# Short token blocks of a mixture-of-experts kernel: the second layer in two halves of 64 columns of the array

## The chip, the cores and the metric

The kernel runs on one core of a Trainium2 chip. The metric is the device time of one execution in microseconds. The core has five engines that run their own instruction streams and wait for each other by semaphores: TensorE (PE in the profile; its weight loads are PEld), VectorE (DVE), ScalarE (ACT), GpSimd (POOL) and SyncE (SP, which here only issues transfers). An engine's sequencer handles register loads, tests and jumps; the profile marks these with a q (PEldq, ACTq).

## What is computed

A linear attention feeds a mixture of experts with one expert per token. Softmaxes of q (over the head dimension) and of k (over the sequence) are multiplied with v; the 8 heads of 64 make rows x of 512. Each of the 8 x 576 = 4608 rows goes through one of 8 experts:

```
out = zeros((B, S, D))
for b in range(B):
    prev_e = -1
    for s in range(S):
        fresh_e = argmax(logits[b, s])
        e = fresh_e if s == 0 or local_gate[b, s] < 0.5 else prev_e
        prev_e = e
        p = softmax(logits[b, s])
        h = maximum(x[b, s] @ w1[e], 0)       # 512 -> 1024
        out[b, s] = p[e] * (h @ w2[e])        # 1024 -> 512
```

With this input five of the experts get rows, 1152, 576, 595, 576 and 1709 of them.

## The kernel before

The first part (to about 170 us) computes the attention and the choice of experts. Then the rows are sorted by expert on the chip and cut into blocks of at most 128 rows of one expert. A block whose expert has no more rows than 64 left is short; a word of the block's `info` says so. There are 38 blocks. Blocks 0 to 5 come from an order written out by hand (`ORDER`, `Plan`), the others from `block(b)` (line 1135), whose Python order is the order of each engine's instructions; the last ones lie in nested conditions (`rest`, line 1174).

Inputs and weights are split in two f16 parts each, high and low, and three products of the four are summed, so that the result is as good as f32. For a block, `gather` fetches the rows, `prep_x`, `prep_hi` and `prep_lo` scale and split them, and `turn_dma` transposes them by a transfer into `xT`. In `block(b)` these last steps work for block b + 3. `ffn1(b, g)`, for g = 0 and 1, makes half of the 1024 hidden values, transposed (`hidden`: 32 matmuls, tokens as columns). In blocks from 6 on it tests the word `few` on TensorE, and a short block streams half the columns. `act_copy`, `act_add`, `act_hi` and `act_lo` (ScalarE, VectorE, ScalarE, VectorE) apply the relu and split the hidden values into `hi` and `lo`. `ffn2(b, g)` (line 905) takes these as the stationary operand, 128 hidden values x 128 tokens, streams 512 columns of `w2h` or `w2l`, and sums 12 matmuls for each g into `py`, one bank of PSUM, of which there is one buffer. `give` (line 911, ScalarE) scales `py` by the row's share `pb` into `ys`, and `put` (POOL) scatters the rows to the output.

When block b + 1 belongs to a new expert, `renew` (line 953) splits that expert's weights, 16 pieces, each with one ScalarE and one VectorE instruction. It stands in a condition (line 954) in both engines' streams, between the steps above: pieces 0 to 9 during block b, 10 to 15 during block b + 1.

The order in `block(b)` that matters here is, with other work left out: `ffn1(b, 0)`, `act(b, 0)`, weight pieces, `ffn2(b - 1, 1)`, `ffn1(b, 1)`, `give(b - 1)`, `put(b - 1)`, weight pieces, `prep_hi` and `prep_lo` of block b + 3, `act(b, 1)`, weight pieces, `ffn2(b, 0)`. So `ffn2(b, 0)` waits until `give(b - 1)` has read `py`.

A condition that tests on one engine makes each other engine jump to the join as well; where two arms raise a semaphore by different counts, the arm with fewer is brought to the larger count.

Of the kernel before, what the change touches and what calls it, by code (L numbers as in the profile page):

```python
# [12 lines left out]
AF = mybir.ActivationFunctionType  # L13
ALU = mybir.AluOpType
AX = mybir.AxisListType
ET = mybir.EngineType
# [3 lines left out]
DM = H * D  # L20
# [11 lines left out]
NA = 6  # L32
# [117 lines left out]
def moe_kernel(ctx, tc, q, k, v, w_gate, w_local, w1, w2, out, dbg=None):  # L150
    nc = tc.nc
# [11 lines left out]
    W, plan = {}, []  # L163
# [3 lines left out]
    gidx, sidx, info = [], [], []  # L167
# [6 lines left out]
    def at(pair, b):  # L174

        return pair[0][:, b] if b < NA else pair[1][:, b - NA]
# [605 lines left out]
    xg, xn, x2, xT, pb, pt, py, hi, lo, hf, ys, ph = ([] for _ in range(12))  # L782
    fst, e0, few, phs = {}, {}, {}, {}
    AHEAD, NPB = 4, 4
# [36 lines left out]
    def word(w_, hi_, engines):  # L821
        return nc.values_load(w_, min_val=0, max_val=hi_, engines=engines,
                              skip_runtime_bounds_check_because="clamped where it is worked out")
# [39 lines left out]
    def ffn1(b, g):  # L863
        if b < NA:
            hidden(b, g, P)
            return
        if g == 0:
            few[0] = word(at(info, b)[:, 5:6], 1, [ET.PE])
        with tc.If(few[0] == 1) as cmp:
            hidden(b, g, P // 2)  # L870
        with cmp.Else():
            hidden(b, g, P)

    def hidden(b, g, n):

        ph_, xT_ = ph[g % len(ph)], xT[b % 4]
        phs[g] = ph_
        for f in range(4):
            fs = slice(P * (4 * g + f), P * (4 * g + f) + P)

            def big(c):
                nc.tensor.matmul(ph_[:, f, :].rearrange("p (i t) -> p i t", i=2)[:, :, 0:n], W["w1h"][:, c, fs], xT_[:, :, c, 0:n],  # L882
                                 start=(c == 0), stop=(c == 3))

            big(0)
            for c in range(4):
                nc.tensor.matmul(ph_[:, f, 0:n], W["w1l"][:, c, fs], xT_[:, 0, c, 0:n], start=False, stop=False)  # L887
            for c in range(1, 4):
                big(c)
# [13 lines left out]
                                       op0=ALU.max, op1=ALU.subtract)  # L903

    def ffn2(b, g):
        hi_, lo_ = hi[b % 2], lo[b % 2]
        for f in range(4 * g, 4 * g + 4):
            for i, (h_, w_) in enumerate(((hi_, W["w2h"]), (hi_, W["w2l"]), (lo_, W["w2h"]))):
                nc.tensor.matmul(py[0], h_[:, f, :], w_[:, f, :], start=(f == 0 and i == 0), stop=(f == 7 and i == 2))  # L909

    def give(b):
        nc.scalar.activation(ys[b % 2], py[0], AF.Copy, scale=pb[b % NPB])  # L912

    def put(b):
        i_, j_ = (sidx[0], b) if b < NA else (sidx[1], b - NA)
# [153 lines left out]
    for b in range(NP + 4):  # L1069
# [28 lines left out]
        for g in range(2):  # L1098
            wp_ = [("Wl", 4 * g + i) for i in range(4)] if b == 0 else [("RN", b, g)]
            add(("F1", b, g), PE, ffn1, after=[("Tc" if b < NT_PE else "D", b)] + wp_, order=[("ow",)] + ([("F2", b - 1, g)] if b else [("F1", 0, 0)] * g)  # L1100
                + ([("F1", b, 0)] if g else []), takes=[("psh", (b, g))], uses=[("xT", b)])
            add(("Ac", b, g), ACT, act_copy, after=[("F1", b, g)], uses=[("psh", (b, g))], takes=[("hf", (b, g))])
            add(("Ad", b, g), DVE, act_add, after=[("Ac", b, g)], uses=[("psh", (b, g)), ("hf", (b, g))])
            add(("Ar", b, g), ACT, act_hi, after=[("Ad", b, g)], uses=[("hf", (b, g))] + ([("hh", b)] if g else []), takes=[] if g else [("hh", b)])
            add(("Al", b, g), DVE, act_lo, after=[("Ar", b, g)], uses=[("hf", (b, g)), ("hh", b)])
            if b == NP - 1 and g:
                continue
            wp_ = [("Wl", 8 + 4 * g + i) for i in range(4)] if b == 0 else [("RN", b, 2 + g)]
            add(("F2", b, g), PE, ffn2, after=[("Al", b, g)] + wp_, order=[("F1", b, 1)] if g == 0 else [("F1", b + 1, 0)],
                takes=[] if g else [("psy", b)], uses=[("hh", b)] + ([("psy", b)] if g else []))  # L1110
        if b < NP - 1:
            add(("Gv", b), ACT, give, after=[("F2", b, 1), ("Gp", b)], uses=[("psy", b), ("pb", b)], takes=[("y", b)])
            add(("Pt", b), POOL, put, after=[("Gv", b)], uses=[("y", b)])
# [21 lines left out]
    def block(b):  # L1135
# [5 lines left out]
        if b + 1 < NBM:  # L1141
            gather_share(b + 1)
            if b + 1 not in fst:
                flag(b + 1)
        ffn1(b, 0)
        act(b, 0)
        renew(b, FROM[b][0])
        next_(b, (0, 1))
        ffn2(b - 1, 1)
        ffn1(b, 1)  # L1150
        give(b - 1)
        put(b - 1)
        renew(b, FROM[b][1])
# [3 lines left out]
        renew(b, FROM[b][2])  # L1157
        next_(b, (4, 5, 6, 7))
        ffn2(b, 0)
        next_(b, (8, 9))  # L1160
        if b + 3 < NBM:
# [24 lines left out]
    def last(b):  # L1186
        ffn2(b, 1)
        give(b)
        put(b)
# [29 lines left out]
```

## Time and profile before

| what | us |
|---|---|
| median of 3 runs | 592.33 |
| lowest and highest | 591.73, 595.31 |
| profiled execution, its time | 594.43 |
| profiled execution, its span | 592.6 |
| mean granted TensorE clock | 0.92 of full |

The span runs from the first to the last instruction. A row of a timeline gives the start from the span's begin, the duration, engine, line, operation, the tiles written and read, shapes as partitions x elements, how many instructions the row merges, and in square brackets how long the engine was idle before it and who ended that. Matmuls overlap, so their step is the difference of starts, not the duration. A granted clock of 1.00 is 2.4 GHz, 0.50 is 1.2 GHz.

### The profile page before, as it was taken

What the parts mean: (1) busy time and instruction counts of PE and PEld (TensorE: products, weight loads), DVE (VectorE), ACT (ScalarE), POOL (GpSimd) and SP (SyncE); (2) the same over time, 40 slices, a digit from 0 to 9 for tenths busy, and PEclk for the clock granted to TensorE, in tenths of its full rate; (3) what the DMA queues carried; (4) which work ended last, traced back from release to release, by engine and by line L of the source; (5) the groups of instructions that cost most, each with busy time, mean ns of one, the idle gap of its engine ahead of it and who ended that gap; (6) DMA issues with size and microseconds to landing.
All of it is one profiled execution on the core that took longest, in us unless ns stands there. A gap on an engine that the chain in (4) does not pass through costs nothing. (4 is left out here: it accounts for less than half of the span.)

```text
span 592.6 us, 15086 instructions
## 1 busy us (share of the span) xinstructions
PE 522.8 (88%) x5558; PEld 371.2 (63%) x5558; DVE 349.1 (59%) x626; ACT 266.2 (45%) x442; POOL 213.1 (36%) x230
## 2 busy tenths in 40 slices
PE   2667886877679999899999899999998999999995
PEld 2456665656556666476576666666665776667762
DVE  3687789889868886335743763474376333333331
ACT  1544345276447353235643743464375333333332
POOL 4132313223611212455344353443534434252441
PEclk9777789576769999799999999999999999999999
DMA  9999989997772454763895499369649924333341
GB/s 234 256 257 219 275 216 266 261 206 174 238 269 43 132 178 143 195 199 104 201 211 113 77 289 140 76 209 211 125 60 262 180 71 108 59 106 68 76 97 48
DMA packets 101297, 98.55 MB, mean 166 GB/s; under 512 B 56255, under 2 KB 84927, under 8 KB 101184
## 3 DMA queue, kind: packets, MB, share of 16 engines
q1 hardware_dynamic: 93536, 74.92, 53.4%
q0 software_dynamic: 7648, 22.20, 14.3%
q8 instruction: 62, 1.02, 0.8%
q14 instruction: 51, 0.42, 0.3%
HBM read 206.76 MB, written 20.89 MB: 384 GB/s over the span
## 5 line engine op out<-in xcount | busy, mean ns | idle before, releaser
L909 PE MATMUL py<-w2h,hi 128*128 128x512 f16 x304 | 116.2, 382 | 7.4 <-ACT y L912 3.5
L909 PE MATMUL py<-w2h,lo 128*128 128x512 f16 x304 | 116.3, 382 | 0.6
L909 PE MATMUL py<-w2l,hi 128*128 128x512 f16 x304 | 116.2, 382 | 0.2 <-DVEq L954 0.2
L882 PEld LDWEIGHTS <-w1h 128*128 128x128 f16 x1216 | 104.2, 98 | 14.3 <-issue 0.3
L916 POOL DMA_INDIRECT out<-y,sidx x38 | 39.2, 1032 | 195.5 <-ACTq L954 138.2
L887 PEld LDWEIGHTS <-w1l 128*128 128x128 f16 x1216 | 91.7, 98 | 14.3 <-issue 0.3
L909 PEld LDWEIGHTS <-hi 128*128 128x128 f16 x608 | 59.0, 98 | 65.7 <-issue 9.3
L882 PE MATMUL ph<-xT,w1h 128*128 128x256 f16 (+1 forms) x624 | 97.7, 270 | 0.0
L882 PE MATMUL pi<-xT,w1h 128*128 128x256 f16 (+1 forms) x592 | 91.8, 268 | 0.0
L902 DVE SCALAR_TENSOR_TENSOR lo<-hf,hi 128x512 f16<-128x512 f32 x76 | 54.8, 721 | 46.1 <-ACTq L954 37.6
L898 ACT ACTIVATE hi<-hf 128x512 f16<-128x512 f32 x76 | 47.8, 629 | 71.0 <-DVE hf L895 68.6
L895 DVE TENSOR_TENSOR hf<-ph,hf 128x512 f32<-128x512 f32 x39 | 26.9, 691 | 70.8 <-ACT hf L892 64.6
L847 DVE SCALAR_TENSOR_TENSOR x<-xn,x 128x512 f16<-128x512 f32 x41 | 35.0, 857 | 45.1 <-ACT x L184 43.5
L887 PE MATMUL ph<-xT,w1l 128*128 128x128 f16 (+1 forms) x624 | 59.6, 218 | 0.0
L892 ACT COPY hf<-ph 128x512 f32<-128x512 f32 x39 | 22.7, 582 | 80.9 <-PE ph L882 71.7
L887 PE MATMUL pi<-xT,w1l 128*128 128x128 f16 (+1 forms) x592 | 55.9, 217 | 0.0
L828 POOL DMA_INDIRECT xg<-xrows,gidx x42 | 45.3, 1077 | 29.2 <-issue 11.6
L909 PEld LDWEIGHTS <-lo 128*128 128x128 f16 x304 | 29.9, 98 | 39.6 <-DVE lo L902 2.4
L834 POOL DMA_INDIRECT pb<-shares,gidx x39 | 43.5, 1116 | 7.9 <-issue 7.6
L839 POOL TENSOR_TENSOR xn<-xg 128x512 f32<-128x512 f32 x35 | 37.3, 1067 | 16.7 <-DMA xg<-xrows,gidx 12.6
L410 POOL TENSOR_TENSOR qs<-qt,qm 128x512 f32<-128x512 f32 x23 | 24.9, 1094 | 49.7 <-DVE qm L404 18.1
L357 PE MATMUL pk<-VP,KT 128*64 128x65 f32 (+1 forms) x640 | 39.9, 280 | 2.7 <-issue 1.9
(223 smaller groups left out, 681.5 us busy)
## 6 DMA issues: line engine op xcount, KB each, us to landing
s<-in_moe_w SPq DMA_DIRECT2D x77, 2048.0 KB
xrows<-xt SPq DMA_DIRECT2D x12, 888.0 KB
qt<-in_q SPq DMA_DIRECT2D x24, 384.0 KB
KT<-in_k SPq DMA_DIRECT2D x16, 512.0 KB
VT<-in_v SPq DMA_DIRECT2D x16, 512.0 KB
s<-in_moe_w SPq DMA_DIRECT2D x4, 1024.0 KB
KT<-in_k SPq DMA_DIRECT2D x8, 128.0 KB
VT<-in_v SPq DMA_DIRECT2D x8, 128.0 KB
```

The source lines that it names most:

```text
L357: nc.tensor.matmul(pkv[64 * i:64 * i + 64, g], KT[b % NKT][ps, 4 * i + g, c], VP[b % 2][ps, 4 * i + g, c], start=(c == 0), stop=(c == KC - 1))
L828: nc.gpsimd.indirect_dma_start(out=xg[b % AHEAD], out_offset=None, in_=src, in_offset=bass.IndirectOffsetOnAxis(ap=i_[:, j_:j_ + 1], axis=0))
L834: nc.gpsimd.indirect_dma_start(out=pb[b % NPB], out_offset=None, in_=src, in_offset=bass.IndirectOffsetOnAxis(ap=i_[:, j_:j_ + 1], axis=0))
L839: eng.tensor_tensor(out=xn[b % 2].rearrange("p (g x d) -> p g x d", g=4, x=2), in0=xg[b % AHEAD].rearrange("p (g x) -> p g x", g=4)[:, :, ...
L847: nc.vector.scalar_tensor_tensor(out=x2[b % 2][:, 1, :], in0=xn[b % 2], scalar=XS, in1=x2[b % 2][:, 0, :], op0=ALU.mult, op1=ALU.subtract)
L882: nc.tensor.matmul(ph_[:, f, :].rearrange("p (i t) -> p i t", i=2)[:, :, 0:n], W["w1h"][:, c, fs], xT_[:, :, c, 0:n], start=(c == 0), stop ...
L887: nc.tensor.matmul(ph_[:, f, 0:n], W["w1l"][:, c, fs], xT_[:, 0, c, 0:n], start=False, stop=False)
L895: nc.vector.tensor_tensor(out=hf[g], in0=phs[g][:, :, 0:P], in1=hf[g], op=ALU.add)
L898: nc.scalar.activation(hi[b % 2][:, 4 * g:4 * g + 4, :], hf[g], AF.Relu)
L902: nc.vector.scalar_tensor_tensor(out=lo[b % 2][:, gs_, :], in0=hf[g], scalar=0.0, in1=hi[b % 2][:, gs_, :], op0=ALU.max, op1=ALU.subtract)
L909: nc.tensor.matmul(py[0], h_[:, f, :], w_[:, f, :], start=(f == 0 and i == 0), stop=(f == 7 and i == 2))
L916: nc.gpsimd.indirect_dma_start(out=outr, out_offset=bass.IndirectOffsetOnAxis(ap=i_[:, j_:j_ + 1], axis=0), in_=ys[b % 2], in_offset=None, ...
```

## The change

In a short block from block 6 on, `ffn2` becomes `result_few`: each matmul is split into two with the same 64 tokens as the stationary operand. One gives output columns 0 to 255 through columns 0 to 63 of the array into partitions 0 to 63 of `py`, the other output columns 256 to 511 through columns 64 to 127 into partitions 64 to 127. `give` then copies the second half from partitions 64 to 127 to the first 64 partitions of `ys`, scales the first half there, and scales the second in place: three ScalarE instructions. The word `few[b]` is now kept per block and loaded on ScalarE too, and `ffn2` (TensorE) and `give` (ScalarE) test it. Full blocks take the old instructions behind these tests. The description of the change also has "rows transposed three blocks ahead"; the diff is this:

```diff
--- before.py
+++ after.py
@@ -865,8 +865,8 @@
             hidden(b, g, P)
             return
         if g == 0:
-            few[0] = word(at(info, b)[:, 5:6], 1, [ET.PE])
-        with tc.If(few[0] == 1) as cmp:
+            few[b] = word(at(info, b)[:, 5:6], 1, [ET.PE, ET.Activation])
+        with tc.If(few[b] == 1) as cmp:
             hidden(b, g, P // 2)
         with cmp.Else():
             hidden(b, g, P)
@@ -903,13 +903,41 @@
                                        op0=ALU.max, op1=ALU.subtract)
 
     def ffn2(b, g):
+        if b < NA:
+            result(b, g)
+            return
+        with tc.If(few[b] == 1) as cmp:
+            result_few(b, g)
+        with cmp.Else():
+            result(b, g)
+
+    def result(b, g):
         hi_, lo_ = hi[b % 2], lo[b % 2]
         for f in range(4 * g, 4 * g + 4):
             for i, (h_, w_) in enumerate(((hi_, W["w2h"]), (hi_, W["w2l"]), (lo_, W["w2h"]))):
                 nc.tensor.matmul(py[0], h_[:, f, :], w_[:, f, :], start=(f == 0 and i == 0), stop=(f == 7 and i == 2))
 
+    def result_few(b, g):
+
+        hi_, lo_ = hi[b % 2], lo[b % 2]
+        for f in range(4 * g, 4 * g + 4):
+            for i, (h_, w_) in enumerate(((hi_, W["w2h"]), (hi_, W["w2l"]), (lo_, W["w2h"]))):
+                for j in range(2):
+                    d_ = slice(DM // 2 * j, DM // 2 * j + DM // 2)
+                    nc.tensor.matmul(py[0][64 * j:64 * j + 64, d_], h_[:, f, 0:64], w_[:, f, d_],
+                                     start=(f == 0 and i == 0), stop=(f == 7 and i == 2))
+
     def give(b):
-        nc.scalar.activation(ys[b % 2], py[0], AF.Copy, scale=pb[b % NPB])
+        if b < NA:
+            nc.scalar.activation(ys[b % 2], py[0], AF.Copy, scale=pb[b % NPB])
+            return
+        with tc.If(few[b] == 1) as cmp:
+            y_, s_, h = ys[b % 2][0:64], pb[b % NPB][0:64], DM // 2
+            nc.scalar.copy(y_[:, h:DM], py[0][64:128, h:DM])
+            nc.scalar.activation(y_[:, 0:h], py[0][0:64, 0:h], AF.Copy, scale=s_)
+            nc.scalar.activation(y_[:, h:DM], y_[:, h:DM], AF.Copy, scale=s_)
+        with cmp.Else():
+            nc.scalar.activation(ys[b % 2], py[0], AF.Copy, scale=pb[b % NPB])
 
     def put(b):
         i_, j_ = (sidx[0], b) if b < NA else (sidx[1], b - NA)
```

## Rows read from the trace of the kernel before

**Rows 1.** The page's first part, TensorE: busy us (share), instructions.

```profile
PE 522.8 (88%) x5558; PEld 371.2 (63%) x5558; DVE 349.1 (59%) x626; ACT 266.2 (45%) x442; POOL 213.1 (36%) x230
```

**Rows 2.** TensorE by line and shape, whole run: count, busy us, mean ns, idle before.

```profile
L909 PE MATMUL py<-w2h,hi 128*128 128x512 f16 x304 | 116.2, 382 | 7.4 <-ACT y L912 3.5 <-ACTq L954 2.7 <-ACT hi L898 0.8
...
L887 PE MATMUL ph<-xT,w1l 128*128 128x64 f16 x48 | 3.4, 193 | 0.0
```

**Rows 3.** Busy us in 420 to 460: PE, PEld, DVE, ACT, POOL; granted clock; DMA share; GB/s.

```profile
420.00:460.00 40.00, 38.16 (x333) 25.07 (x332) 24.29 (x36) 22.95 (x40) 16.57 (x16) 1.00 0.60 149
```

**Rows 4.** TensorE in order of time, 434 to 455: start, us, what [idle before].

```profile
434.02 0.38 PE L909 MATMUL py<-w2h,hi 128*128 128x512 f16 x1
...
436.61 0.27 PE L882 MATMUL ph<-xT,w1h 128*128 128x256 f16 x1
...
439.25 0.38 PE L909 MATMUL py<-w2h,hi 128*128 128x512 f16 x1
...
444.15 0.49 PE L882 MATMUL pi<-xT,w1h 128*128 128x256 f16 x3
446.01 0.38 PE L909 MATMUL py<-w2h,hi 128*128 128x512 f16 x1 [1.36 <-ACT y L912]
...
451.61 0.39 PE L909 MATMUL py<-w2h,hi 128*128 128x512 f16 x1 [0.21 <-ACT hi L898]
...
454.50 0.27 PE L882 MATMUL pi<-xT,w1h 128*128 128x256 f16 x1
```

**Rows 5.** ScalarE in order of time, 428 to 460.

```profile
430.02 0.59 ACT L892 COPY hf<-ph 128x512 f32<-128x512 f32 x1 [1.98 <-PE ph L882]
...
441.41 0.56 ACT L892 COPY hf<-ph 128x512 f32<-128x512 f32 x1
...
445.27 0.69 ACT L912 ACTIVATE y<-py,pb 128x512 f32<-128x512 f32 x1 [0.21 <-ACTq L954]
```

**Rows 6.** VectorE in order of time, 420 to 465.

```profile
438.06 0.69 DVE L902 SCALAR_TENSOR_TENSOR lo<-hf,hi 128x512 f16<-128x512 f32 x1 [0.70 <-ACTq L954]
439.06 2.50 DVE L938 SCALAR_TENSOR_TENSOR w1l<-s,w1h 128x512 f16<-128x512 f32 x4 [0.30 <-ACT w1h L184]
```

**Rows 7.** ScalarE in order of time, a plain block.

```profile
478.75 0.58 ACT L892 COPY hf<-pi 128x512 f32<-128x512 f32 x1 [1.38 <-PE pi L882]
```

**Rows 8.** TensorE in order of time, 54 to 62, array in 64x64 tiles.

```profile
58.83 0.62 PE L434 MATMUL px<-R,qe 64*64 64x74 f32 x24 [2.57 <-issue]
```

**Rows 9.** ScalarE by line and shape, the one of 256 columns.

```profile
L382 ACT ACTIVATE kvT<-pq 128x256 f16<-128x256 f32 x8 | 3.0, 381 | 10.7 <-PE pq L378 10.6
```

**Rows 10.** TensorE in order of time, 237 to 250.

```profile
239.21 0.49 PE L882 MATMUL pi<-xT,w1h 128*128 128x256 f16 x3
242.44 0.59 PE L909 MATMUL py<-w2h,hi 128*128 128x512 f16 x1 [2.73 <-ACTq L954]
```

**Rows 11.** Busy us and granted clock in four windows of 4 us (columns as in rows 3).

```profile
56.00:60.00 4.00, 1.43 (x50) 1.17 (x50) 2.60 (x4) 1.10 (x2) 1.19 (x2) 1.00 1.12 204
240.00:244.00 4.00, 1.41 (x4) 0.38 (x4) 2.29 (x3) 1.93 (x4) 2.33 (x2) 0.71 0.47 90
244.00:248.00 4.00, 4.00 (x11) 1.45 (x10) 1.20 (x2) 0.63 (x1) 1.07 (x2) 0.50 0.81 158
248.00:252.00 4.00, 4.00 (x39) 3.19 (x37) 0.32 (x1) 0.58 (x1) 1.88 (x2) 0.93 0.82 228
```

**Rows 12.** TensorE in order of time, the end.

```profile
583.60 0.39 PE L909 MATMUL py<-w2h,lo 128*128 128x512 f16 x1
...
585.55 0.38 PE L909 MATMUL py<-w2h,lo 128*128 128x512 f16 x1
```

**Rows 13.** ScalarE in order of time, the end.

```profile
586.03 0.69 ACT L912 ACTIVATE y<-py,pb 128x512 f32<-128x512 f32 x1 [3.20 <-PE py L909]
```

**Rows 14.** Line 822 on ScalarE's sequencer: ns min/median/max, first and last start.

```profile
L822 ACTq TENSOR_LOAD <-info x41: 273/285/772, 183.8 to 583.4; - x41
```

**Rows 15.** Line 869 on TensorE's sequencer (columns as in rows 14).

```profile
L869 PEldq COMPARE_BRANCH  x70: 63/210/877, 244.5 to 579.3; - x70
```


## The prediction

> **What bounds it now.** The page's first part puts TensorE at 88% of the span [rows 1]. The shapes of TensorE's matmuls give the size of what is changed: the second layer's three lines hold 304 matmuls each, 912 in all, which is 38 blocks of 24; the 64-column form of the first layer appears 48 times for ph, at 16 a block, so just 3 of the 38 blocks are short [rows 2]. Blocks 0 to 5 have no test, so 29 of the other 32 take the full arm.
>
> Next come the stretches around those three. The 64-column matmuls lie at about 323, 428 and 575 us. I read the middle block; the first shows the same rows 105.8 us earlier. In 420 to 460 TensorE works 38.16 of 40 us [rows 3]; the question is what ends the missing 1.84. The order of time on TensorE tells it [rows 4]: the short block's twelve second-layer matmuls run from 434.02 to 436.61 (2.59 us, 0.216 each) with no wait, but the next block's first half, which could start when the matmuls of 444.15 are through at about 444.5, begins at 446.01 behind "ACT y L912", the short block's own `give`: 1.5 us (1.36 from their modelled end). From there to 454.50 three stages take 8.49 us, where 2.59 for a half and 2.64 for the first layer (436.61 to 439.25) make 7.82: another 0.67 us of waits, at 451.61 and behind it. Is that `give` late because TensorE was late? ScalarE's rows say no [rows 5]: since 430.02, where it waited for the short block's first layer, it has hardly waited for TensorE; the copy at 441.41 starts without idle time though its matmuls ended about 2 us before. It is converting the next expert's weights, with VectorE, which does the same [rows 6]. So from 430 to 452 this pair sets the time and TensorE waits. Elsewhere TensorE sets it: in a plain block ScalarE idles 1.38 us for it [rows 7].
>
> **The change, part by part.**
>
> *The matmuls.* In a short block 24 matmuls of 512 columns become 48 of 256, two per old one in different column halves. If the halves run together, a pair costs 256 columns, 0.216/2 = 0.108 us, and a block saves 12 x 0.108 x 2 = 2.59 us. If they run in turn a pair costs 0.216 and nothing is saved; with each half's weight load uncovered too (0.10 each), about 0.41, twice the old time. I take 0.108, because this trace has tiled matmuls that overlap: 24 of 64x64 tiles with 74 columns took 0.62 us [rows 8], 1776 columns, 2.9 per ns, where the 512-column row streams 2.4 per ns. Switching tile shapes four times a block has no row; 0 to 0.2 us each, in time TensorE waits anyway.
>
> *The same block's `give`.* One ScalarE instruction becomes three of 256 columns and a test. The nearest row of 256 columns is 0.381 us [rows 9] against 0.69 for the old `give` [rows 5]. Overlapped they add 0.1, strictly in a row 3 x 0.381 + a test - 0.69, some 0.66; the third reads what the first wrote, so I take 0.45. Queued behind it are the next weight pieces, the next rows' conversion and the copy of the first layer; waiting for it are TensorE's next second layer and POOL's store.
>
> *What the saved time meets.* In the two transitions (after the short blocks at 323 and 428) the saving is not on the path. Replaying it on [rows 4 to 6]: the first half ends at 435.3; the next block's first layer follows to 438.0; the second half waits for its lo (438.06 + 0.69) and ends at about 439.9; the first layer's second half wants the weight pieces finished 439.7 to 441.6 and ends near 442.6. TensorE then idles until `give`, at 446.01 + 0.45 = 446.46: 3.8 us instead of 1.5.
>
> *What the longer wait does to the clock.* An idle of 2.73 us before 242.44 [rows 10] was followed by half clock, 1.2 GHz: the granted clock is 0.71, 0.50 and 0.93 of full in the three windows of 4 us from 240 on [rows 11], so some 2.3 + 4.0 + 0.6 = 6.9 us at half, of which about 6.1 lay on matmuls. That cost 3.05 us. Waits of 1.5 us at the two transitions left it at full; one of 2.57 us did too [rows 8, 11]. I take 3.8 us to fall on the former side. Each transition then: + 0.45 (`give`) + 3.05 (clock) - 0.67 (the later waits, which the slowed matmuls now run past) = + 2.83; two, + 5.7 us.
>
> *The last short block.* Its first half gains nothing: the second half's start hangs on lo, at 583.60 [rows 12]. From there nine steps of 0.216 lead to the last pass at 585.55; at 0.108 they save 0.97. The last `give` [rows 13] and its store follow with nothing beside them, so + 0.45 counts, and + 0.05 for a test ahead of the `give` before: - 0.5 us.
>
> *The tests.* In 29 full blocks two more tests on TensorE, one on ScalarE, a register load there (0.285 us median) [rows 14] and jumps on every queue, SP's and POOL's too. TensorE's sequencer already does 70 such tests at 0.21 us median, 0.88 at most [rows 15], and [rows 3, 4] are still filled with matmuls but for the waits above: the queued matmuls hide them. ScalarE's are covered by the 1.38 us of [rows 7]. Zero; without that cover 58 x 0.21 = 12.2 us. SP and POOL only jump, while idle.
>
> "Rows transposed three blocks ahead" moves nothing: `block` already does so, and no line of the diff touches it.
>
> **Sum.** + 5.7 - 0.5 = + 5.2 us. Against the profiled execution (594.43 us, span 592.6 and 1.8 around it) that is 599.6; that execution lies 2.1 over the median of 592.33, so I predict 592.33 + 5.2 = **597.5 us**, 0.9% slower. With the half clock lying on 4.1 to 6.6 us of work and `give` at 0.1 to 0.66, this case spans 594.4 to 599.5.
>
> **Rivals.**
> *The halves run in turn, or the clock stays* (the change does not do what it says, or TensorE's longer wait is harmless). For it: the one wait of 2.57 us without a fall. Then the transitions pay only `give`, 2 x 0.45, and the end + 0.5 at worst: 592.5 to 593.7, say 593.5. The Trainium skill, TensorEngine Tiling (Array Packing), Restrictions and Gotchas, says that column tiling excludes Fast Weight Load; if slower loads then ate the gain this case would follow, by its rule 593.5 where my sum has 597.5. No row has that load in f16.
> *The saving reaches the end*: 3 x 2.59 = 7.8 us, 584.6, faster. It decides if ScalarE's `give` was itself held by TensorE's second layer. For it: 88% busy. Against: [rows 5], where nothing before `give` waits on it.
> *TensorE's sequencer runs dry* at the new tests in the full blocks: 58 x 0.21 = 12.2 us, 604.5. Point: the queued first-layer matmuls (some 0.04 us per instruction) must last shorter than a test. Against: 70 tests now without a gap.
>
> **Chances.** Forecast 0.60, clock or halves 0.20, saving reaches the end 0.08, sequencer 0.12. About 1% (5.9 us) is what a measurement of this kernel can tell from no change. Slower by over 1% means above 598.25: the sequencer case and a fourth of the forecast, 0.27; faster by over 1%: most of the third case, 0.06; within: 0.67. The range 591 to 600.5 holds the first two cases and leaves out most of the last two.
>
> **What would show it.** In the changed trace: 48-matmul short blocks with a step near 0.054 us per matmul; three ScalarE instructions in their `give`; TensorE idle of 3.5 to 4 us behind that `give` in the two blocks after; granted clock 0.50 in the 6 us that follow; a last lo-to-last-pass of about 1.0 us; no new gaps in plain blocks. The forecast is wrong if the clock stays at full after those waits, if the wait before `give` shortens in step with the matmuls, or if gaps appear at the tests.

## The result, and the profile after

The changed kernel takes 596.35 us (median of 20 runs, 592.15 to 601.88) beside 590.23 us for the kernel before (20 runs on the same chip, 587.06 to 595.31): a ratio of **1.0099, 95% interval 1.0074 to 1.0125**, or + 5.8 us (4.4 to 7.4) where + 5.2 was forecast. This ratio and all that follow compare fast runs alone, so they are not the quotients of the medians. The time came out; the terms of the sum did not, and most of this text is about that.

A word on method first. The runs of each of these two kernels spread over 8 us and more, and the first 258 us of the eleven profiled executions lie up to 12 us apart, in kernels whose program there is nearly the same. So the traces are compared from 258 us on: the start of a TensorE matmul in one trace, minus the start of the same matmul in the trace of before. That offset is constant to 0.04 us over whole plain blocks and jumps at a few places, and the jumps are the cost. Each trace is one execution of its kernel. For this kernel it is - 1.22 us at 258 us and, for the last store, 592.45 - 586.99 = + 5.46: **+ 6.68 us**, in six jumps.

The page's first part of the kernel after, against [rows 1]:

```profile
PE 521.8 (87%) x5630; PEld 375.1 (63%) x5630; DVE 348.2 (58%) x626; ACT 268.3 (45%) x448; POOL 217.7 (36%) x230
```

TensorE's second layer by line and shape, against [rows 2] (count, busy us, mean ns, idle time ahead and who ended it): the 912 matmuls of 512 columns are now 840, with 144 of 256.

```profile
L918 PE MATMUL py<-w2h,hi 128*128 128x512 f16 x280 | 107.8, 385 | 15.7 <-ACT y L938 8.3 <-ACTq L982 5.0 <-ACT y L940 2.0
...
L927 PE MATMUL py<-w2h,hi 128*64 128x256 f16 x48 | 7.0, 277 | 2.1 <-ACTq L982 1.8
```

TensorE in order of time around the second short block, against [rows 4] (the start, the duration, what it is, the idle time ahead of it):

```profile
442.42 0.28 PE L927 MATMUL py<-w2h,lo 128*64 128x256 f16 x2
...
442.53 0.28 PE L927 MATMUL py<-w2h,hi 128*64 128x256 f16 x2
...
443.28 0.28 PE L882 MATMUL pi<-xT,w1h 128*128 128x256 f16 x1
...
450.25 0.38 PE L918 MATMUL py<-w2h,hi 128*128 128x512 f16 x1 [4.16 <-ACT y L938]
...
454.24 0.42 PE L882 MATMUL ph<-xT,w1h 128*128 128x256 f16 x1
...
457.16 0.38 PE L918 MATMUL py<-w2h,hi 128*128 128x512 f16 x1
...
459.75 0.27 PE L882 MATMUL pi<-xT,w1h 128*128 128x256 f16 x1
```

A pair of halves steps by 0.11 us: they run at once. TensorE then idles 4.16 us for `give`, where it idled 1.36. The second layer behind the wait takes 454.24 - 450.25 = 3.99 us instead of 2.59, and the later wait of 0.21 is gone. The granted clock in those windows, which answers to [rows 11], says why (columns: window, its length, busy us of PE, PEld, DVE, ACT and POOL, granted clock, DMA share, GB/s):

```profile
341.00:345.00 4.00, 3.73 (x11) 1.41 (x11) 3.00 (x3) 2.36 (x5) 3.17 (x3) 0.65 1.00 403
345.00:349.00 4.00, 4.00 (x38) 3.04 (x37) 3.05 (x5) 1.67 (x3) 1.25 (x1) 0.93 0.65 196
450.00:454.00 4.00, 3.75 (x12) 1.49 (x12) 3.02 (x3) 2.35 (x5) 3.16 (x3) 0.68 1.02 399
454.00:458.00 4.00, 4.00 (x38) 3.08 (x36) 3.02 (x5) 1.67 (x3) 1.25 (x1) 0.90 0.81 218
```

A mean of 0.65 between levels of 1.00 (2.4 GHz) and 0.50 (1.2 GHz) is 2.8 of 4 us at half, 0.93 another 0.6: 3.4 us at half behind each of the two waits, where 6.9 had been counted in [rows 11].

ScalarE's `give` there, against [rows 5]: three instructions for one, and a longer idle time ahead of them.

```profile
447.19 1.13 ACT L184 ACTIVATE w2h<-s 128x512 f16<-128x512 f32 x2
448.94 0.37 ACT L936 COPY y<-py 64x256 f32<-64x256 f32 x1 [0.62 <-ACTq L982]
449.34 0.47 ACT L937 ACTIVATE y<-py,pb 64x256 f32<-64x256 f32 x1
449.71 0.49 ACT L938 ACTIVATE y<-y,pb 64x256 f32<-64x256 f32 x1
```

What the forecast did not have at all lies at the two changes of expert behind full blocks. TensorE before (first fence) and after (second), the second layers at the two waits of one such change, and the last store on POOL:

```profile
287.97 0.38 PE L909 MATMUL py<-w2h,hi 128*128 128x512 f16 x1 [0.39 <-ACT y L912]
...
299.11 0.38 PE L909 MATMUL py<-w2h,hi 128*128 128x512 f16 x1
...
586.99 1.00 POOL L916 DMA_INDIRECT out<-y,sidx  x1 [5.91 <-POOLq L1178]
```

```profile
287.26 0.38 PE L918 MATMUL py<-w2h,hi 128*128 128x512 f16 x1 [0.90 <-ACT y L940]
...
299.17 0.38 PE L918 MATMUL py<-w2h,hi 128*128 128x512 f16 x1 [0.60 <-ACTq L982]
...
592.45 1.00 POOL L944 DMA_INDIRECT out<-y,sidx  x1 [5.43 <-POOLq L1206]
```

No matmul of that block is different, yet its next second layer waits 0.51 us longer and the one after that 0.6 us where it did not wait. The tests on the two sequencers, against [rows 15] (ns min/median/max):

```profile
L869 ACTq COMPARE_BRANCH  x70: 38/45/50, 243.3 to 584.6; - x70
...
L909 PEldq COMPARE_BRANCH  x70: 63/207/370, 249.5 to 589.6; - x70
L909 ACTq COMPARE_BRANCH  x70: 34/45/50, 257.7 to 590.2; - x70
...
L934 ACTq COMPARE_BRANCH  x35: 34/45/45, 262.9 to 591.3; - x35
L934 PEldq COMPARE_BRANCH  x35: 63/205/338, 263.8 to 590.0; - x35
```

The word of `few[b]` is loaded for both engines, so **both execute every test**, ScalarE those of the first and second layer too, in which it has nothing to do: five a block in its stream, besides the load. In the kernel before, line 869 has such records on TensorE alone. An engine that does not test has none at these lines, before or after: the jumps that the section on the kernel before and the prediction put on every other engine are not in the traces.

The jumps of the offset, of all traces of this study, in us (read as said above, places by the time in the trace of before; "full" and "short": the change of expert behind such a block, both of its waits; "stalls" are explained with the fillers):

| kernel | full, 288 | short, 340 | full, 394 | short, 446 | 460 to 580 | end | stalls | sum |
|---|---|---|---|---|---|---|---|---|
| changed kernel | 1.28 | 2.00 | 1.20 | 1.99 | 0.42 | -0.21 | | 6.68 |
| tests alone | 1.21 | 0.94 | 1.16 | 0.95 | 0.25 | 0.27 | | 4.78 |
| tests, give in three | 1.27 | 1.81 | 1.22 | 1.97 | 0.42 | 0.71 | | 7.40 |
| changed, fillers | 1.29 | 1.81 | 1.22 | 1.63 | 0.45 | -0.21 | 2.80 | 8.99 |
| word loaded twice | 0.42 | 1.62 | 0.41 | 0.60 | 0.09 | -0.63 | | 2.51 |
| the same, TensorE tests at give | 0.42 | 1.62 | 0.41 | 2.44 | 0.08 | -0.25 | | 4.72 |
| word twice, fillers | 0.41 | 0.62 | 0.40 | 0.61 | 0.09 | -0.62 | 6.43 | 7.94 |
| halves in the last blocks alone | 0 | 0 | 0 | 0 | 0.10 | -0.62 | | -0.52 |
| before, new order | 0.27 | 1.58 | 0.70 | 1.59 | 0.54 | -0.14 | | 4.54 |
| word twice, new order | 0.62 | 2.46 | 1.23 | 2.46 | 0.33 | -0.52 | | 6.58 |

### The profile page after: what moved, and what is told of

It reads as the page before. It is cut to its first block, busy times and chain, and to the rows that moved or that the text cites. A ratio compares the mean times of both kernels' runs of the same rounds, so it can differ in the third digit from the quotient of the medians.

```text
span 598.4 us, 15576 instructions
## 1 busy us (share of the span) xinstructions
PE 521.8 (87%) x5630; PEld 375.1 (63%) x5630; DVE 348.2 (58%) x626; ACT 268.3 (45%) x448; POOL 217.7 (36%) x230
## 3 DMA queue, kind: packets, MB, share of 16 engines
q8 instruction: 75, 1.23, 0.9%
## 5 line engine op out<-in xcount | busy, mean ns | idle before, releaser
L918 PE MATMUL py<-w2h,hi 128*128 128x512 f16 x280 | 107.8, 385 | 15.7 <-ACT y L938 8.3
L918 PE MATMUL py<-w2h,lo 128*128 128x512 f16 x280 | 108.4, 387 | 0.2
L918 PE MATMUL py<-w2l,hi 128*128 128x512 f16 x280 | 108.0, 386 | 0.4 <-DVEq L982 0.4
L918 PEld LDWEIGHTS <-hi 128*128 128x128 f16 x560 | 54.9, 99 | 70.4 <-issue 17.2
L834 POOL DMA_INDIRECT pb<-shares,gidx x39 | 50.0, 1283 | 9.8 <-issue 7.3
L918 PEld LDWEIGHTS <-lo 128*128 128x128 f16 x280 | 27.7, 99 | 35.8 <-issue 2.8
L357 PE MATMUL pk<-VP,KT 128*64 128x65 f32 (+1 forms) x640 | 45.1, 303 | 1.7 <-issue 0.9
L357 PEld LDWEIGHTS pk<-VP,KT 128*64 128x64 f32 (+1 forms) x640 | 36.8, 200 | 10.8 <-issue 4.6
```

The costliest lines, as they stand in the source:

```text
L357: nc.tensor.matmul(pkv[64 * i:64 * i + 64, g], KT[b % NKT][ps, 4 * i + g, c], VP[b % 2][ps, 4 * i + g, c], start=(c == 0), stop=(c == KC - 1))
L834: nc.gpsimd.indirect_dma_start(out=pb[b % NPB], out_offset=None, in_=src, in_offset=bass.IndirectOffsetOnAxis(ap=i_[:, j_:j_ + 1], axis=0))
```

## The experiments

**1. The tests alone.** The new tests stay, the old arms stand behind them.

```
         with tc.If(few[b] == 1) as cmp:
-            result_few(b, g)
+            result(b, g)
...
         with tc.If(few[b] == 1) as cmp:
-            y_, s_, h = ys[b % 2][0:64], pb[b % NPB][0:64], DM // 2
-            nc.scalar.copy(y_[:, h:DM], py[0][64:128, h:DM])
-            nc.scalar.activation(y_[:, 0:h], py[0][0:64, 0:h], AF.Copy, scale=s_)
-            nc.scalar.activation(y_[:, h:DM], y_[:, h:DM], AF.Copy, scale=s_)
+            nc.scalar.activation(ys[b % 2], py[0], AF.Copy, scale=pb[b % NPB])
```

> The changed kernel with all its new tests, but with the old arms behind them: the short blocks run the full second layer and the old one-instruction give. Theory A (a test that ScalarE executes holds up its stream where TensorE waits for it; the word is tested on ScalarE at all three places, since it is loaded for both engines): about +0.55 us at each of the four expert changes behind full blocks (2.4 in sum), +0.4 to +0.5 at each of the two changes behind short blocks, +0.2 at the end, together +3.2 to +3.6 us over the kernel before; the clock behind the short blocks stays at full, with waits of about 2 us there. Rival B (the tests are hidden, as I forecast; halves, give and clock make the whole loss of 5.8): within 0.5 us of the kernel before. Rival C (TensorE's sequencer pays for the tests in every full block): offsets that grow in plain blocks, up to +12 us.

Measured: + 4.78 us in the trace, about 1.2 at a change behind a full block and 0.95 behind a short one, with nothing in plain blocks. The rows of TensorE, the two waits behind a full block and then the first behind a short one:

```profile
287.02 0.38 PE L918 MATMUL py<-w2h,hi 128*128 128x512 f16 x1 [0.84 <-ACT y L937]
...
298.91 0.38 PE L918 MATMUL py<-w2h,hi 128*128 128x512 f16 x1 [0.60 <-ACTq L979]
...
448.37 0.38 PE L918 MATMUL py<-w2h,hi 128*128 128x512 f16 x1 [1.81 <-ACT y L935]
```

They are the waits of the changed kernel behind the full block, though no second layer and no `give` was changed. The clock stayed at 1.00 behind the waits of 1.81 us. So in the traces the tests alone are most of the loss from 258 us on, and B and C fall there. The table repeats it: behind full blocks each change costs 1.16 to 1.29 us in the four kernels in which ScalarE executes all the tests, about 0.4 in the three of the same order in which it executes one a block, and nothing in the one that has none there. The times do not bear this out: the ratio is 1.0013 (0.9979 to 1.0047), - 1.2 to + 2.8 us for the whole program, so by the times B is not excluded. The rest may have gone in the stretch before 258 us, where the executions differ by more than this, or the one execution in the trace may not stand for the others; no run here shows which.

**2. The tests, and give in three instructions**, with the short blocks' second layer whole.

```
-            nc.scalar.copy(y_[:, h:DM], py[0][64:128, h:DM])
+            nc.scalar.copy(y_[:, h:DM], py[0][0:64, h:DM])
...
-            result_few(b, g)
+            result(b, g)
```

> As the kernel of the tests alone, and with the short blocks' give in three instructions, but their second layer whole as before (the give reads the whole result's rows 0 to 63). Theory A: the three instructions add 0.55 to 0.6 us at each of the two changes behind short blocks, wait of TensorE before the next second layer about 2.5 us, clock still at full there; about +1.2 us over the kernel of the tests alone, +4.5 to +4.9 over the kernel before. Rival B (my forecast's terms: give 0.45 each, tests 0): +1.0 to +1.4 over the kernel before. Rival D (the wait of 2.5 us already drops the clock): some 1.0 to 1.7 us more at each of the two places.

Measured: ratio 1.0102 (1.0053 to 1.0152), + 7.40 us in the trace. TensorE's resumption behind the short blocks moves by 0.44 and 0.41 us against experiment 1 (offset steps of 0.88 and 0.86 against 0.44 and 0.45): that is the price of the three instructions, not the 0.55 to 0.6 I had put down for theory A. And the clock fell at both places, as rival D had it, after waits of 2.25 and 2.23 us, though beside the price of `give` the two changes cost 0.43 and 0.61 us more than in experiment 1, not the 1.0 to 1.7 of D:

```profile
447.67 0.42 PE L918 MATMUL py<-w2h,hi 128*128 128x512 f16 x1 [2.23 <-ACT y L938]
```

```profile
447.00:451.00 4.00, 3.33 (x9) 1.27 (x9) 2.60 (x3) 2.77 (x6) 2.78 (x3) 0.61 1.02 408
451.00:455.00 4.00, 4.00 (x39) 2.98 (x38) 3.30 (x5) 1.67 (x3) 1.65 (x2) 0.96 1.13 227
```

At the two changes behind short blocks this kernel loses 1.81 and 1.97 us, the changed kernel 2.00 and 1.99. So **the halves themselves do next to nothing there**: they lengthen TensorE's wait from 2.2 to 4.2 us, and the clock falls either way. Their gain shows at the end alone: + 0.71 here, - 0.21 in the changed kernel, 0.92 us in the last half.

**3. Fillers in the wait.** Twelve matmuls of 512 columns into a spare tile behind the second half of the first two short blocks; nothing reads them.

```
+        for i in range(12 if fill else 0):
+            nc.tensor.matmul(spare[0], hi_[:, 4, :], W["w2h"][:, 4, :], start=(i == 0), stop=(i == 11))
```

> The changed kernel with 12 more matmuls of 512 columns into a spare tile behind the second half of the first two short blocks: they compute nothing that is used, 12 x 0.216 = 2.6 us of TensorE in the time that it waits. Theory A (the halves' own harm is the clock that falls after the long wait): the wait shrinks from 4.2 to about 1.6 us, the granted clock stays at full behind it, each of the two transitions ends 0.9 to 1.3 us earlier than in the changed kernel: -1.8 to -2.6 us against it, +3.2 to +4.0 over the kernel before. Rival B (the clock costs the 3.05 us each that I forecast): -6 against the changed kernel. Rival D (the clock's fall costs nothing since the waits that follow swallow it): no change against it, +5.8.

Measured: ratio 1.0121 (1.0071 to 1.0172). The waits shrank to 1.57 us and the clock stayed at 1.00, as A said, but the two changes cost 1.81 and 1.63 us, only 0.2 and 0.4 less than in the changed kernel: nearly D. (At the first place the second wait is also 0.3 us longer than in experiment 1, for which I have no cause.) The offsets in between show why. In the changed kernel the half clock adds 1.64 and 1.39 us, but then the two waits that follow (0.4 to 0.6 us in sum, forecast as 0.67) and the second wait for the tests (0.49 in experiment 1) are run past. With the clock at full those are all back. Net, the clock is worth 0.2 to 0.6 us a place here, by this experiment and by the one before.

The kernel was slower over all, by 2.80 us at two places in plain blocks that no theory had. The larger is a wait of 2.32 us:

```profile
362.46 0.49 PE L882 MATMUL pi<-xT,w1h 128*128 128x256 f16 x3
365.27 0.39 PE L918 MATMUL py<-w2h,hi 128*128 128x512 f16 x1 [2.32 <-ACTq L984]
```

```profile
L909 PEldq COMPARE_BRANCH  x70: 63/207/3675, 251.9 to 591.0; - x70
```

The wait is put down to a semaphore of ScalarE. But all that this matmul needs from ScalarE was there: `give` had started at 360.76 and took 0.69 us. A test of TensorE's that began at 361.5 us took 3.675 us, 18 times the median, and ended at 365.2, just ahead of this matmul. It is my third rival (TensorE's sequencer runs dry), at one test; the smaller place, 0.3 us, follows a test of 1.52 us at 472.65.

**4. The word loaded twice**, once for each engine, so that ScalarE tests at `give` only and TensorE at the two layers only.

```
-            few[b] = word(at(info, b)[:, 5:6], 1, [ET.PE, ET.Activation])
+            few[b] = word(at(info, b)[:, 5:6], 1, [ET.PE])
+            short[b] = word(at(info, b)[:, 5:6], 1, [ET.Activation])
...
     def give(b):
-        with tc.If(few[b] == 1) as cmp:
+        with tc.If(short[b] == 1) as cmp:
```

> The changed kernel with its word loaded twice, once for TensorE alone (its two tests) and once for ScalarE alone (the test of give): ScalarE no longer executes the two tests of the second layer. Theory A (tests that ScalarE executes cost about 0.6 us a change of expert, and it is those of the second layer as well as the one of give): the extra waits at the four changes behind full blocks fall from 0.6 to about 0.2 us each, -1.5 to -2 us against the changed kernel, +4 over the kernel before. Rival E (only the test of give itself counts, since it alone stands directly ahead of give): no change against the changed kernel, +5.8. Rival C (the second load of the word costs ScalarE what the tests saved): +5.8 or a little more.

Measured: the two changes behind full blocks cost 0.42 and 0.41 us instead of 1.28 and 1.20, about 0.2 for each of their waits, as A had it; the sum in the trace is + 2.51, below the + 4 expected, since the places behind the short blocks gained too. The ratio is 1.0077 (1.0042 to 1.0113), 2.5 to 6.7 us: again it agrees with the trace at one end only. In the trace E and C fall. ScalarE's idle time ahead of `give` behind the short block:

```profile
452.95 1.13 ACT L184 ACTIVATE w2h<-s 128x512 f16<-128x512 f32 x2
454.33 0.37 ACT L937 COPY y<-py 64x256 f32<-64x256 f32 x1 [0.24 <-ACTq L983]
```

It is 0.24 us, where it was 0.62 with the tests of the layers in the stream. Behind the first full block, the same `give` in the kernel before, the changed kernel and this one:

```profile
287.23 0.69 ACT L912 ACTIVATE y<-py,pb 128x512 f32<-128x512 f32 x1 [0.21 <-ACTq L954]
...
286.53 0.69 ACT L940 ACTIVATE y<-py,pb 128x512 f32<-128x512 f32 x1 [0.72 <-PE pi L882]
...
294.04 0.69 ACT L941 ACTIVATE y<-py,pb 128x512 f32<-128x512 f32 x1 [0.42 <-ACTq L983]
```

With none of the new tests ahead of it ScalarE is idle 0.21 us, with three (second layer, first layer, `give`) 0.72, with one 0.42: 0.15 to 0.21 us a test, though a test's own record is 45 ns. The second row names a first-layer matmul as what ended the wait; but in the kernel before that stage ends only at 287.58 us, after this `give` has started, so `give` does not need it. The 0.51 us between the first two rows is what TensorE waits longer there in the changed kernel. And the clock gave an answer that no theory had. TensorE's two waits are alike, and the granted clock is not:

```profile
347.84 0.47 PE L919 MATMUL py<-w2h,hi 128*128 128x512 f16 x1 [3.77 <-ACT y L939]
...
455.64 0.38 PE L919 MATMUL py<-w2h,hi 128*128 128x512 f16 x1 [3.78 <-ACT y L939]
```

```profile
347.00:351.00 4.00, 3.16 (x8) 1.15 (x8) 2.61 (x4) 2.93 (x6) 2.61 (x3) 0.62 0.95 382
...
455.00:459.00 4.00, 3.36 (x22) 1.89 (x22) 2.63 (x3) 2.73 (x6) 2.82 (x3) 1.00 1.00 396
```

Behind the first the clock fell and the change cost 1.62 us; behind the second it stayed and the change cost 0.60.

**5. The same, with TensorE's test at give put back**, to tell what the split had saved: ScalarE's tests of the two layers or TensorE's test at `give`.

```
-            short[b] = word(at(info, b)[:, 5:6], 1, [ET.Activation])
+            short[b] = word(at(info, b)[:, 5:6], 1, [ET.PE, ET.Activation])
```

> As the kernel with the word loaded twice, but the word for give is loaded for TensorE too, so TensorE executes a test at give again, as in the changed kernel, while ScalarE still has no test at the second layer. It tells whether the 0.85 us that came back at each change behind a full block belonged to ScalarE's two tests or to TensorE's one. Theory A (ScalarE's): the waits behind full blocks stay at 0.4 us over before for each change, +2.5 to +3.5 from 258 us to the end. Rival F (TensorE's test at give): 1.2 to 1.3 us for each change as in the changed kernel, +4.3 or more.

Measured (one run, 598.58 us, so only its trace is read): 0.42 and 0.41 us behind the full blocks, as without that test. So it was **ScalarE's tests of the two layers**; F falls. The sum in the trace is 4.72, above the range given, and the 2.2 us over experiment 4 lie elsewhere: 1.84 at the second short block, where the clock now fell already within the wait, and 0.38 at the end, for which I have no cause.

```profile
449.07 0.58 PE L919 MATMUL py<-w2h,hi 128*128 128x512 f16 x1 [3.78 <-ACT y L939]
```

```profile
447.00:451.00 4.00, 1.93 (x5) 0.69 (x5) 2.70 (x5) 3.55 (x9) 1.40 (x2) 0.54 0.84 285
451.00:455.00 4.00, 4.00 (x19) 1.82 (x18) 3.21 (x3) 1.36 (x3) 3.03 (x3) 0.60 0.94 356
```

A third outcome of the same wait: (1 - 0.54)/0.5 x 4 + (1 - 0.60)/0.5 x 4 = 6.9 us at half, and the second layer behind it 2.5 us longer.

**6. The word twice, and the fillers.**

> The kernel with the word loaded twice, plus the 12 unused matmuls of 512 columns behind the second half of the first two short blocks. In the two traces without them the four waits of 3.8 us left the transitions at +1.6, +1.6, +2.4 (the clock fell behind the wait) and +0.6 us (it did not). Theory A (what differs between those is the clock alone): the waits shrink to about 1.2 us, the granted clock stays at 1.00 behind both, and both transitions come to +0.6 us; from 258 us to the end +1.5 us (0.4 for each change behind a full block, 0.6 for each behind a short one, -0.5 at the end). Rival H (the spread has another cause, a late piece or a late store): +0.6 at the one and +1.6 or more at the other, with the clock at full.

The edit is that of experiments 3 and 4 together. Measured: both waits 1.19 us, the clock at 1.00 behind both, and **0.62 and 0.61 us** at the two changes. Theory A holds, H falls: what differed between 0.60, 1.62 and 2.44 us was the clock. Here, without the waits for the layers' tests to run past, a fall of the same length as in the changed kernel costs 1.0 us net (1.62 - 0.62), and the longer one 1.8. The other columns come to the + 1.5 expected. But the ratio is 1.0089 (1.0060 to 1.0117), and the trace has 6.43 us more at three places in plain blocks. The largest, 4.38 us with the half clock behind it:

```profile
361.22 0.61 PE L919 MATMUL py<-w2h,hi 128*128 128x512 f16 x1 [2.89 <-ACTq L985]
```

```profile
L910 PEldq COMPARE_BRANCH  x70: 63/210/4510, 247.2 to 586.5; - x70
```

Again a test of TensorE's: it began at 356.7 us, took 4.51 and ended with this wait. It is the same matmul as in experiment 3: its start in the trace of before is 361.82 us in both cases. The other two places, 0.95 and 1.10 us, lie in the middle of a stage with no test at them:

```profile
308.71 0.34 PE L888 MATMUL ph<-xT,w1l 128*128 128x128 f16 x3 [0.78 <-issue]
```

There TensorE waited for nothing that the profile shows. In the nine traces without fillers the longest test of TensorE took 1.20 us, but for one: the last record of this kind in TensorE's stream, behind its last matmul, takes 3.30 us in the kernel before (line 1178), 3.96 in the changed kernel and 3.4 to 4.6 in the others, and costs nothing there. So a long one needs no fillers. The fillers make the short arm longer by twelve instructions; that this is the reason was not tried.

**7. Give ahead of the weight pieces.** The kernel before, with another order in the block and nothing else.

```
         act(b, 0)
-        renew(b, FROM[b][0])
         next_(b, (0, 1))
...
         put(b - 1)
+        renew(b, FROM[b][0])
         renew(b, FROM[b][1])
         next_(b, (2, 3))
-        prep_b(b + 3)
         act(b, 1)
+        prep_b(b + 3)
```

> The kernel before with its order changed and nothing else: in a block, the conversion of weight pieces 10 and 11 is put behind give and the store of the block before, and the conversion of the next rows behind the second half's activation. Theory A (at a change of expert it is ScalarE's order that makes TensorE wait for give): the waits of 1.37 and 0.39 us go, as far as the moved pieces do not hold the second layer in their place; between -1.5 and -5 us. Rival G (the pieces bind instead: the second layer reads piece 10 after six of its matmuls, 1.3 us on): the wait moves to the middle of the second layer and the time stays within 1 us.

Measured: ratio 1.0098 (1.0063 to 1.0132), slower than either theory allowed. The wait for `give` behind the first short block does shrink, from 1.37 to 0.56 us, but the weights are now late ahead of it. ScalarE, and the matmul that waits for it, in the block before:

```profile
328.86 1.15 ACT L184 ACTIVATE w1h<-s 128x512 f16<-128x512 f32 x2 [1.71 <-DMA s<-in_moe_w]
...
329.92 0.67 ACT L912 ACTIVATE y<-py,pb 128x512 f32<-128x512 f32 x1
...
330.64 0.38 PE L909 MATMUL py<-w2h,hi 128*128 128x512 f16 x1 [1.89 <-ACTq L954]
```

The conversion of the next pieces waits 1.71 us for the DMA that brings them, and `give` stands behind it. So the order cannot simply be turned round. G is right that something else binds, but it is the load, not the second layer's pieces.

**8. The word twice, and that order.**

> The changed kernel with the word loaded twice and with that new order. Theory A (tests and give cost what they do since they stand on ScalarE ahead of TensorE's next second layer): with give earlier by the 1.1 us of the two pieces, the wait behind the short blocks falls from 3.8 to about 2.7, that behind full blocks to zero, the clock perhaps stays; 0 to -3 us against the kernel before. Rival G (the pieces bind): +2 to +4 us.

The edit is that of experiments 4 and 7 together. Measured: ratio 1.0150 (1.0099 to 1.0201), + 6.58 us in the trace, with 2.46 us at each change behind a short block. That is outside both theories. It confirms 7 and adds nothing.

**9. Halves in the last blocks alone.** The two arms and the three-instruction `give` only from block 36 on, the word loaded twice.

```
     def ffn2(b, g):
-        if b < NA:
+        if b < NBF:
...
     def give(b):
-        if b < NA:
+        if b < NBF:
```

> The halves where their matmuls lie on the path alone: the second layer of the last six blocks (those that may be empty or short) has the two arms and give its three instructions, with the word loaded twice, and all earlier blocks run the second layer and give of the kernel before, without a test. Theory A (a last short block gains the 0.97 us of its matmuls and pays 0.4 for give): no step at the four changes of expert at 288 to 457 us, and -0.5 to -0.7 us at the end. Rival I (the tests of the last six blocks, all on one path, cost as much): 0 to +0.5 us. Less than the times can tell; read from the trace.

Of the blocks that the edit takes in, two run (not six, as I had written), with two tests and a jump on ScalarE. Measured: no jump anywhere between 258 and 575 us, and - 0.52 us at the end, as theory A had it; the last half runs from 580.69 (its first lo pair) to its last pair at 581.70 in 1.01 us, where [rows 12] have 1.95: 0.94 of the 0.97 saved, and `give` takes 0.4 of it back. The ratio is 0.9976 (0.9938 to 1.0015): this version is ahead of the changed kernel, but it can't be told from the kernel before.

```profile
580.69 0.30 PE L929 MATMUL py<-w2h,lo 128*64 128x256 f16 x2 [0.32 <-DVEq L984]
...
581.70 0.28 PE L929 MATMUL py<-w2h,lo 128*64 128x256 f16 x2
```

## Why the prediction was right, and where it was not

The number was right by luck, by two errors that nearly cancel: in the trace the tests cost 4.7 us more than forecast, and the clock some 3.7 less. By its own signs the forecast was wrong: it named gaps at the tests as one, and they are there. (As a time, 597.5 lies 1.1 us over the measured one: the median of the three runs that it started from, 592.33, is 2.1 us over that of the twenty.)

- **The matmuls**: right. Pairs at 0.108 to 0.11 us, no cost of switching to be seen. The Trainium skill, TensorEngine Tiling (Array Packing), Restrictions, excludes Fast Weight Load with column tiling; if slower loads follow from that, they show nowhere in these steps.
- **give + 0.45 us**: right in size, 0.44 and 0.41 (experiment 2 against 1), and 0.44 at the end.
- **What the saved time meets**: right. The wait is 4.16 us where 3.8 was forecast; the 0.4 more is the tests.
- **The clock, + 3.05 - 0.67 each**: the fall came, at half the size. It lay on 3.4 us of work, so it cost 1.64 and 1.39 us, and what it ran past was larger, as the tests had made more waits. Net 0.2 to 0.6 where I had 2.38. I took one stretch [rows 11] for the length of all; the same wait of 3.8 us has given none, 3.4 and 6.9 us at half.
- **The tests, zero**: the step that failed. They cost 4.78 us in the trace of experiment 1, most of the loss from 258 us on; the times of that experiment, - 1.2 to + 2.8 us, do not confirm so much. I covered ScalarE's by the 1.38 us that it waits for TensorE in a plain block [rows 7], and in plain blocks that held. At a change of expert it is TensorE that waits for ScalarE, as [rows 5] had shown me in the same text, and there is no cover. I also counted one test on ScalarE and two more on TensorE, where the word's load for two engines put five in ScalarE's stream and three more in TensorE's.
- **The end, - 0.5**: the matmuls gave 0.92 of 0.97, `give` took 0.44 of 0.45; the tests took 0.25 and 0.27 where I had 0.05. With the word loaded twice it was - 0.6.
- **The range of the forecast's case**: its upper end of 599.5 does not follow from its terms. With 3.3 us for the clock and 0.66 for `give`, two changes add 2 x (0.66 + 3.3 - 0.67) and the end takes 0.3 off, which gives 598.6.

| term | forecast | measured |
|---|---|---|
| tests | 0.05 | 4.78 (1) |
| give, two changes and the end | 1.35 | 1.29 (2 less 1) |
| half clock, net of what it runs past, two places | 4.76 | about 1.0 (2 less 1, rest of the two places) |
| halves, the last block | -0.97 | -0.92 (changed less 2) |
| halves at the two changes, and small rest | 0 | about 0.5 |
| sum | 5.2 | 6.68 in the trace, 5.8 (4.4 to 7.4) in the times |

Of the rivals, the halves in turn did not happen, and the clock stayed at full behind two waits of 1.8 us and one of 3.78. The saving reached the end in the last block alone. The sequencer did not run dry in the changed kernel, and did so in the two kernels with fillers.

What stays open: why the times of experiments 1 and 4 stand in the opposite order to their traces, and so how much of the loss in the times is the tests'; why some tests of the filler kernels take microseconds; and the 0.38 us at the end of experiment 5.

## What to carry to other kernels

Cover is a matter of place: before calling an added instruction free, find the stretch where its engine is the one waited for, and price it there. When a condition's word is loaded for several engines, look whether each of them executes every test; load it once for each engine that acts on it. Faster matmuls ahead of a wait for another engine only lengthen the wait; they paid where TensorE's chain was the end, 0.92 us of 7.8.

## What the runs showed of the hardware

- **One wait, three outcomes of the clock**: idle times of 3.77 and 3.78 us on TensorE behind the same work were followed by 3.4 us (twice), none and 6.9 us at half clock; waits of 2.25 and 2.23 were followed by a fall, of 1.81 (twice) by none. The Trainium skill, TensorE: Matmul & The Clock Gate, Part 1, says that the number of matmuls at the low clock varies between runs of one kernel, which it tells of the kernel's start; no two traces here are of one kernel, but behind a wait the two places of one trace (experiment 4, 3.4 us and none) differ as much.
- **Half clock can be cheap**: 1.64 us of slower matmuls came to 0.2 to 0.6 net in the changed kernel, as they ran past waits that followed; where fewer waits followed (experiment 4 beside 6), 1.0.
- **A short test is not a short stop**: ScalarE's tests take 45 ns each in their records, but one ahead of a `give` lengthens ScalarE's idle time from 0.21 to 0.42 us and three to 0.72; the two layers' tests make TensorE wait about 0.4 us more at each of the two waits of a change of expert (1.28 - 0.42 for both).
- **TensorE's tests have a tail**: 207 ns median, but 3.7 and 4.5 us at most in the two kernels with a longer short arm, at the same matmul, and 3.3 to 4.6 for the last one in every trace.
